# A feed-forward weight loaded in four column chunks instead of three, and two steps of the start put in another order

## The chip, the cores and the metric

The kernel runs on one core of a Trainium2 chip. The metric is the device time of one execution in microseconds (us); smaller is better. Engines are named as the profile names them: PE (TensorE matmul), PEld (its weight load), DVE (VectorE), ACT (ScalarE), POOL (GpSimd) and SP (SyncE). SPq, ACTq and POOLq are the instruction queues of those engines where they issue DMAs.

## The reference

`x` is 8 sequences of 4096 positions with 192 channels. The first step is a causal convolution along the sequence: the 192 channels are 8 heads of 24, each head has 7 taps, and the taps are softmaxed. The second step is a feed-forward layer over all 32768 rows, 192 to 2048 to 192, with an ELU between the two products.

```python
w = weight - np.max(weight, axis=-1, keepdims=True)
w = np.exp(w)
w = w / (np.sum(w, axis=-1, keepdims=True) + 1e-09)
x_pad = np.concatenate([np.zeros((B, K - 1, D), np.float32), x], axis=1)
x_unf = x_pad[:, np.arange(S)[:, None] + np.arange(K)[None, :], :].reshape(B, S, K, H, D // H)
att = np.einsum('hk,bskhg->bshg', w, x_unf).reshape(B * S, D)
h = att @ w_in                                     # 32768 x 2048
g = np.where(h > 0, h, np.exp(np.minimum(h, 0)) - 1)
out = g @ w_out                                    # 32768 x 192
```

`x`, `w_in` and `w_out` are float32 in DRAM. The kernel computes in 16-bit types with float32 accumulation; the DMAs that POOL issues convert while they load.

## The kernel before, in words

The 32768 rows are cut into 32 superblocks of 1024 rows, each of them two groups of 512. The hidden 2048 columns are cut into 16 strips `q` of 128 columns. One *pair* `n` is strip `q = n % 16` of superblock `s = n // 16`.

**One pair.** PE makes six matmuls into one of three slots of `H` (L646): three contraction steps `j` for each of the two groups `r`. The 192 channels are held as 3 times 64, and group 0 sits on partitions 0 to 63, group 1 on 64 to 127, so `w_in` has to be on chip twice, in the lower 64 partitions and in the upper 64. ACT takes the exponential of both groups (L437), POOL clamps it (L354), DVE makes `max(e - 1, h)` as `gT` (L500). A slot of `H` is free again when DVE is through, so PE is at most three slots ahead. A pair of PE instructions on zeroes (`warm_pair`, L537) stands before most pairs of the first superblock. The second product (L676) of superblock `t` is placed in the steps from pair `16 * (t + 1) - 1` on: in superblock 0 PE has nearly nothing to do but the pairs.

**The convolution.** For superblocks 1 on, PE multiplies windows of `x` (`xg`) by a band matrix of the taps, `Tr` (L619), ACT copies the result to `csb` (L417), SP writes it to DRAM (L713) and reads it back in the layout `att` that the pairs want (`read_att`, L279). The first two of these steps, `m = 0` and `m = 1`, stand in PE's order behind pairs 5 and 9; for them ACT copies the second half of the result only after the exponentials of the next pair (`late`). Pair 16 is the first that reads `att` from this way.

**The start.** Superblock 0 takes a shorter way, on chip. SP and ACT load the first 1024 rows as float32, `xf` (L249). ACT casts the first half to `xh` (L373, `s_xha`), DVE the second half (L482, `s_xh`). Meanwhile DVE has softmaxed the taps, PE spreads them over the partitions (L549, `s_wb`), and DVE multiplies them with a mask into seven diagonals `Dg` (L475, `s_D`). PE transposes `xh` (L556, L568), ACT and DVE copy the transposed blocks to `xT` (L375, L382, L484), PE applies the diagonals to `xT` (L588), ACT and DVE copy the result to `att` (L385, L391, L486, L491), and pair 0 can start. PE fills the time up to L549 with `WARM[0]` = 11 matmuls on zeroes (L532).

**The weight `w_in`.** It comes in chunks of columns (`WCOLS`), and `Q_PART` says which chunk strip `q` needs. Chunk 0 (columns 0 to 255, strips 0 and 1) is loaded from DRAM twice, once into each half of the partitions. Chunk 1 (256 to 1023, strips 2 to 7) and chunk 2 (1024 to 2047, strips 8 to 15) are loaded once, into the lower 64 partitions, by POOL's queue (L312, semaphores `s_w[1]`, `s_w[2]`); when such a chunk has landed, SP copies it to the upper 64 partitions with an on-chip DMA (L704, semaphores `s_wc`). PE waits for `s_w[0]`, or for the copy's semaphore, ahead of the first strip of each chunk.

**Queues.** POOL issues all converting loads one after the other before its first clamp: `w_in` chunk 0 twice, chunk 1, `xg` of superblock 1 in two parts (L307, parts 1 and 2), chunk 2, `xg` of superblock 2 part 1, the whole of `w_out` (L343), `xg` of superblock 2 part 2. SP issues in program order, and a wait holds everything behind it: the taps, one half of `xf`, the taps to DRAM (L695), the band `Tr` from them (L697), the two copies of `w_in`, then for `m = 0`: the write of `csb` (L713) and three reads of `att` (L279), then the same for `m = 1`, and so on through the kernel.

The order of PE, ACT and SP in the main part is one list, `order`, made when the program is built; it is the same before and after.

Of the kernel before, what the change touches and what calls it, by code (L numbers as in the profile page):

```python
# [12 lines left out]
P = 128  # L13
HP = 64
# [13 lines left out]
NE = 4  # L28
NG3 = 2
LAG = -1  # L30
WCOLS = ((0, 256), (256, 1024), (1024, 2048))
Q_PART = (0,) * 2 + (1,) * 6 + (2,) * 8
WARM = (11, 1)
HALF_STEPS = (10, 10, 6, 6, 10, 11, 11)

CONV_AT = ((4, 1, 1), (12, 2, 0))
# [15 lines left out]
def bass_lightweight_conv__then__act_elu_kernel(  # L52
# [55 lines left out]
    for n in range(NP + NQ + LAG):  # L108
        s, i = divmod(n, NQ)
# [25 lines left out]
    with ExitStack() as stack:  # L135
# [6 lines left out]
        def sema(name):  # L142
            return stack.enter_context(nc.semaphore(name))

        xh = sbuf("xh", [P, 2, QUAD, D], BF16)
# [24 lines left out]
        H = psum("H", [P, 3, 2 * GS])  # L170
        ops = psum("ops", [P, 2, GS])

        s_w = [sema(f"s_w{i}") for i in range(4)]
        s_wd = sema("s_wd")
        s_xl = [sema(f"s_xl{i}") for i in range(2)]
        s_xh = sema("s_xh")
        s_xha = sema("s_xha")
        s_wp = sema("s_wp")
        s_wb = sema("s_wb")
        s_wc = [sema(f"s_wc{i}") for i in range(2)]  # L180
        s_id = sema("s_id")
        s_one = sema("s_one")
        s_z0 = sema("s_z0")
# [99 lines left out]
        @block.gpsimd  # L283
        def _gpsimd(g: bass.BassGpSimd):
            W = Waits(g)

            def load_x(s, part):
                b, t0 = s % NXB, s * SUP
                first = s % SPB == 0
                if part == 0 and not first:  # L290
                    return
                if part == 0:
                    W(s_x[b][0], x_need[s, 0])
                    g.memset(xg[0:PAD, b, 0, :], 0.0).then_inc(s_z)
                    return
                if s > NXB:
                    W(s_cv, 2 * (s - NXB))
                if part == 1:
                    w0, w1, row = 0, XW, t0 - PAD
                else:  # L300
                    w0, w1, row = XW, NWIN, t0 + SUP - P - CW * (NWIN - 1 - XW)
                src = bass.AP(
                    tensor=x_flat.tensor,
                    offset=row * D,
                    ap=[[D, P], [CW * D, w1 - w0], [1, D]],
                )
                g.dma_start(xg[:, b, w0:w1, :], src).then_inc(s_x[b][part - 1], 16)  # L307

            def load_w_in(k, halves):
                c0, c1 = WCOLS[k]  # L310
                for r in halves:
                    g.dma_start(  # L312
                        w_in[HP * r : HP * (r + 1), :, c0:c1],
                        moe_w_in.rearrange("(p j) f -> p j f", j=3)[:, :, c0:c1],
                    ).then_inc(s_w[k], 16)

            W(s_one, 1)
            g.affine_select(
                out=ident[:],
                in_=ident[:],  # L320
                pattern=[[-1, P]],
                compare_op=ALU.is_equal,
                fill=0.0,
                base=0,
                channel_multiplier=1,
            ).then_inc(s_id)
            g.affine_select(
                out=sel[:].rearrange("p (r h c) -> p r h c", r=2, h=HEADS),
                in_=sel[:].rearrange("p (r h c) -> p r h c", r=2, h=HEADS),
                pattern=[[0, 2], [-1, HEADS], [0, 8]],  # L330
                compare_op=ALU.is_equal,
                fill=0.0,
                base=0,
                channel_multiplier=1,
            ).then_inc(s_id)
            W(s_wd, 16)
            load_w_in(0, (0, 1))
            load_w_in(1, (0,))
            for part in (1, 2):
                load_x(1, part)  # L340
            load_w_in(2, (0,))
            load_x(2, 1)
            g.dma_start(  # L343
                w_out[:, :, :], moe_w_out.rearrange("(q p) d -> p q d", p=FC)
            ).then_inc(s_w[3], 16)
            load_x(2, 2)
            for n in range(NP):
                s, i = divmod(n, NQ)
                for at, part in X_AT:
                    if at == i and s and s + NXB < NS:  # L350
                        load_x(s + NXB, part)
                for u in range(2):
                    W(s_exp, 2 * n + u + 1)
                    g.tensor_scalar(  # L354
                        out=E[:, n % NE, u, :],
                        in0=E[:, n % NE, u, :],
                        scalar1=1.0,
                        scalar2=0.0,
                        op0=ALU.min,
                        op1=ALU.max,  # L360
                    ).then_inc(s_clp)
# [85 lines left out]
        @block.vector  # L447
        def _vector(v):
            W = Waits(v)
            v.memset(zw[:], 0.0).then_inc(s_zw)  # L450
            v.memset(sel[:], 1.0)
            v.memset(ident[:], 1.0).then_inc(s_one)
            v.memset(xT[0:HP, :, :, 0:HALO], 0.0).then_inc(s_z0)
            v.memset(Dg[:, ::8, :], 0.0).then_inc(s_z0)
            v.memset(zt[:], 0.0).then_inc(s_z0)
            W(s_id, 1)
            v.tensor_tensor(mask[:], ident[:, 0:HP], ident[:, HP:P], ALU.add).then_inc(s_v)
            W(s_wd, 16)
            v.tensor_reduce(whm[:], wh[:], AXIS.X, ALU.max).then_inc(s_v)
            W(s_v, 2)  # L460
            v.tensor_scalar(
                out=wh2[:], in0=wh[:], scalar1=whm[:, 0:1], scalar2=None, op0=ALU.subtract
            ).then_inc(s_v)
            W(s_de, 1)
            v.reciprocal(whr[:], whs[:]).then_inc(s_v)
            W(s_v, 4)
            v.tensor_scalar(
                out=zt[:, CW - 1 : CW - 1 + KSIZE],
                in0=whe[:],
                scalar1=whr[:, 0:1],  # L470
                scalar2=None,
                op0=ALU.mult,
            ).then_inc(s_wp)
            W(s_wb, 1)
            v.tensor_tensor(  # L475
                Dg[:, 1:8, :],
                mask[:, :].unsqueeze(1).to_broadcast([P, KSIZE, HP]),
                H[:, 2, 0:KSIZE].unsqueeze(2).to_broadcast([P, KSIZE, HP]),
                ALU.mult,
            ).then_inc(s_D)  # L480
            W(s_xl[1], 16)
            v.tensor_copy(xh[:, 1, :, :], xf[:, 1, :, :]).then_inc(s_xh)  # L482
            W(s_tp, 3)
            v.tensor_copy(xT[:, 1, :, HALO : HALO + P], xt_bank(1)).then_inc(s_xtd)  # L484
            W(s_hc, 2)
            v.tensor_copy(  # L486
                att[:, 0, 1, :].rearrange("p (r t) -> p r t", r=2),
                H[:, 2, :].rearrange("p (r t) -> p r t", r=2)[:, :, 0 : GS // 2],
            ).then_inc(s_hd)
            W(s_hc, 3)  # L490
            v.tensor_copy(  # L491
                att[:, 0, 2, GS // 2 : GS], H[:, 0, GS : GS + GS // 2]
            ).then_inc(s_hd)
            for n in range(NP):
                s, q = divmod(n, NQ)
                if s >= NG3:
                    W(s_mm2, 2 * (s - NG3 + 1))
                for u in range(2):
                    W(s_clp, 2 * n + u + 1)
                    v.scalar_tensor_tensor(  # L500
                        out=gT[:, s % NG3, q, u, :],
                        in0=E[:, n % NE, u, :],
                        scalar=1.0,
                        in1=H[:, slot_of_pair[n] % 3, GS * u : GS * (u + 1)],
                        op0=ALU.subtract,
                        op1=ALU.max,
                    ).then_inc(s_tt)
            b = (2 * NS - 1) % 2
            W(s_mm2, 2 * NS)
            W(s_out[b], 32 * (NS - 1))  # L510
            v.tensor_copy(  # L511
                osb[:, b, 1, :, :].rearrange("p k d -> p (k d)"),
                H[:, last_slot % 3, GS : GS + 2 * D],
            ).then_inc(s_od)

        @block.tensor
        def _tensor(pe):
# [83 lines left out]
            for item in order:  # L601
# [26 lines left out]
                elif item[0] == "h":  # L628
# [5 lines left out]
                    elif n < NQ - 1 and not any(n - 2 <= e < n for e in EARLY_CONV):  # L634
                        conv_read(W, sum(e < n for e in EARLY_CONV) - 1)
                        warm_pair(WARM[1])
                    if Q_PART[q]:
                        W(s_wc[Q_PART[q] - 1], 16)
                    else:
                        W(s_w[0], 32)  # L640
                    W(s_att[s % 2], 16 * NDMA_ATT * ((s + 1) // 2))
                    k = slot_of_pair[n]
                    wait_slot(k)
# [10 lines left out]
                    ins.then_inc(s_h)  # L654
                else:
                    _, t, half, r0, r1 = item
                    W(s_w[3], 16)
                    if (t, half) == last_half:
                        acc = H[:, last_slot % 3, :].rearrange("p (g t) -> p g t", g=2)
                        if r0 == 0:  # L660
# [29 lines left out]
        def _sync(sy):  # L690
# [7 lines left out]
                Tr[:, :, :],  # L698
                bass.AP(tensor=taps.tensor, offset=0, ap=[[1, P], [ZW, HEADS], [1, CW]]),
            ).then_inc(s_band, 16)  # L700
            for k in (1, 2):
                c0, c1 = WCOLS[k]
                W(s_w[k], 16)
                sy.dma_start(  # L704
                    w_in[HP:P, :, c0:c1], w_in[0:HP, :, c0:c1]
                ).then_inc(s_wc[k - 1], 16)

            for item in order:
                if item[0] == "c":
# [52 lines left out]
```

## Time and profile before

| | us |
|---|---|
| median of four runs | 755.67 |
| lowest and highest | 754.07, 756.96 |
| the profiled execution, own time | 754.83 |
| its span (first to last instruction) | 753.1 |
| PE busy | 739.2 (98%) |
| ACT, POOL, DVE busy | 646.7, 658.5, 635.9 |
| L646 and L676 on PE, share of the chain that ended last | 44% each |

About 1.7 us of the profiled execution's own time lie outside the span. The span runs from 0; all places below are microseconds from there. In the list of busy time a row gives the source line, the engine, the operation, the tile written and the tiles read, how many there are, where the first starts and how long they cover. An entry in square brackets is the time in which the engine stood idle before, and what ended it.

### The profile page before, as it was taken

Reading aid. Unit: us, or ns where it says so; the run is one execution under the profiler, and the core shown is the slowest. Engines: PE = TensorE matmul, PEld = TensorE weight load, DVE = VectorE, ACT = ScalarE, POOL = GpSimd, SP = SyncE. Lnnn points to the kernel's source line nnn. Section 1 sums busy time; section 2 is a strip of 40 time slices with the busy share of each in tenths; the row PEclk is TensorE's granted clock in tenths of the full one; section 3 lists DMA queues with packets and bytes.
Section 4 is the critical chain, followed back from the end, with each engine's and each line's share of the span. In section 5 each row is a group of like instructions: output and inputs, shape, how many; then the busy total and the mean of one; then the engine's idle time right before and its main releaser. Section 6 shows DMA issues by size and latency. Waiting matters only on the chain.

```text
span 753.1 us, 32225 instructions
## 1 busy us (share of the span) xinstructions
PE 739.2 (98%) x13860; PEld 512.4 (68%) x13860; DVE 635.9 (84%) x1041; ACT 646.7 (86%) x1163; POOL 658.5 (87%) x1104
## 2 busy tenths in 40 slices
PE   6899999999999999999999999999999999999997
PEld 3366666667667667667667667767767767767676
DVE  3888898888898898898898898888888888888893
ACT  3888888888888888888888888888888888889882
POOL 5888898898998998998998998998998998998882
PEclk9999999999999999999999999999999999999999
DMA  9435345344345344345344345354355354355112
GB/s 178 101 86 109 81 101 117 78 102 98 92 102 114 78 103 95 95 102 113 78 105 95 92 104 111 77 107 93 90 108 110 74 111 92 88 112 106 59 44 64
DMA packets 106590, 72.79 MB, mean 97 GB/s; under 512 B 44488, under 2 KB 105808, under 8 KB 106448
## 3 DMA queue, kind: packets, MB, share of 16 engines
q1 hardware_dynamic: 66432, 54.77, 24.0%
q0 software_dynamic: 39600, 15.39, 19.1%
q8 instruction: 108, 1.77, 1.0%
q10 hardware_dynamic: 416, 0.59, 0.2%
q14 instruction: 34, 0.28, 0.1%
HBM read 44.00 MB, written 41.42 MB: 113 GB/s over the span
## 4 chain that ended last, share of the span: by engine, by line
PE 94%; DMA 2%; ACT 1%; DVE 1%; issue 0%; POOL 0%; SPq 0%
PE H L646 44%; PE ops L676 44%; PE H L619 5%; DMA w_in<-w_in 1%; DMA w_in<-in_moe_w_in_dram 1%; ACT E L437 1%; PE H L676 1%; DVE gT L500 1%; DMA att<-conv_slots 0%; DMA conv_slots<-csb 0%; ACT csb L417 0%; POOL w_in L312 0%; POOL E L354 0%; SPq L279 0%; PE ops L537 0%
## 5 line engine op out<-in xcount | busy, mean ns | idle before, releaser
L500 DVE SCALAR_TENSOR_TENSOR gT<-E,H 128x512 f16<-128x512 f32 x1024 | 630.5, 682 | 96.4 <-POOL E L354 88.5
L354 POOL TENSOR_SCALAR E<-E 128x512 f32<-128x512 f32 x1024 | 603.8, 612 | 79.4 <-ACT E L437 76.1
L437 ACT ACTIVATE E<-H 128x512 f32<-128x512 f32 x1024 | 546.1, 605 | 84.8 <-PE H L646 71.2
L676 PEld LDWEIGHTS ops<-w_out,gT 64*128 64x128 f16 x8064 | 342.1, 94 | 109.7 <-ACT osb L408 10.9
L676 PE MATMUL ops<-w_out,gT 64*128 64x192 f16 x8064 | 414.6, 243 | 0.9 <-DVE gT L500 0.9
L646 PE MATMUL H<-att,w_in 64*128 64x512 bf16 x3072 | 408.5, 378 | 5.1 <-DMA w_in<-w_in 2.4
L646 PEld LDWEIGHTS H<-att,w_in 64*128 64x128 bf16 x3072 | 130.3, 94 | 106.3 <-DVE gT L500 4.7
L417 ACT ACTIVATE csb<-H 128x1024 bf16<-128x1024 f32 x60 | 61.4, 1024 | 0.0
L408 ACT ACTIVATE osb<-ops 128x768 f32<-128x768 f32 x63 | 51.5, 817 | 5.1 <-PE ops L676 5.1
L307 POOL DMA_DIRECT2D xg<-in_x_dram x62 | 52.1, 841 | 0.4 <-issue 0.4
L619 PE MATMUL H<-Tr,xg 128*24 128x122 bf16 (+1 forms) x2400 | 39.3, 209 | 0.0
L619 PEld LDWEIGHTS H<-Tr,xg 128*24 128x24 bf16 x2400 | 30.1, 92 | 9.5 <-issue 9.5
L511 DVE COPY osb<-H 128x384 f32<-128x384 f32 x1 | 0.6, 558 | 8.9 <-PE H L676 8.9
L532 PE MATMUL ops<-zw 128*128 128x512 bf16 x11 | 4.5, 594 | 1.2 <-DVE zw L450 1.2
L676 PE MATMUL H<-w_out,gT 64*128 64x192 f16 x128 | 5.6, 243 | 0.1
L537 PE MATMUL ops<-zw 64*128 64x512 bf16 x20 | 4.4, 429 | 1.2 <-ACT csb L417 1.2
L676 PEld LDWEIGHTS H<-w_out,gT 64*128 64x128 f16 x128 | 5.2, 94 | 0.3 <-PE H L676 0.3
L400 ACT ACTIVATE osb<-H 128x384 f32<-128x384 f32 x1 | 0.5, 491 | 4.7 <-PE H L676 4.7
L532 PEld LDWEIGHTS ops<-zw 128*128 128x128 bf16 x11 | 1.5, 145 | 3.7 <-issue 2.5
L486 DVE CAST att<-H 128x512 bf16<-128x512 f32 x1 | 0.7, 692 | 3.3 <-PE H L588 3.3
L537 PEld LDWEIGHTS ops<-zw 64*128 64x128 bf16 x20 | 1.1, 105 | 3.4 <-ACT csb L417 2.2
L375 ACT ACTIVATE xT<-H 64x24 bf16<-64x24 f32 x1 | 0.2, 188 | 3.2 <-PE H L556 3.2
(46 smaller groups left out, 32.3 us busy)
## 6 DMA issues: line engine op xcount, KB each, us to landing
out_dram<-osb SPq DMA_DIRECT2D x127, 192.0 KB, 2.7
conv_slots<-csb SPq DMA_DIRECT2D x62, 256.0 KB, 2.5
att<-conv_slots SPq DMA_DIRECT2D x186, 64.0 KB
xg<-in_x_dram POOLq DMA_DIRECT2D x31, 240.0 KB, 5.1
xg<-in_x_dram POOLq DMA_DIRECT2D x31, 192.0 KB, 4.5
w_out<-in_moe_w_out_dram POOLq DMA_DIRECT2D x1, 768.0 KB, 16.4
xf<-in_x_dram ACTq DMA_DIRECT2D x1, 384.0 KB, 3.1
xf<-in_x_dram SPq DMA_DIRECT2D x1, 384.0 KB, 3.6
```

What stands on the lines that cost most here:

```text
L307: g.dma_start(xg[:, b, w0:w1, :], src).then_inc(s_x[b][part - 1], 16)
L354: g.tensor_scalar(out=E[:, n % NE, u, :], in0=E[:, n % NE, u, :], scalar1=1.0, scalar2=0.0, op0=ALU.min, op1=ALU.max,).then_inc(s_clp)
L408: a.activation(osb[:, b, :, :, :].rearrange("p g k d -> p g (k d)"), ops[:, :, 0 : 2 * D], ACT.Copy,).then_inc(s_oev)
L417: return a.activation(csb[:, m % 4, b0:b1, :], conv_bank(m)[:, b0:b1, :], ACT.Copy)
L437: a.activation(E[:, n % NE, u, :], H[:, k, GS * u : GS * (u + 1)], ACT.Exp).then_inc(s_exp)
L486: v.tensor_copy(att[:, 0, 1, :].rearrange("p (r t) -> p r t", r=2), H[:, 2, :].rearrange("p (r t) -> p r t", r=2)[:, :, 0 : GS // 2],).the ...
L500: v.scalar_tensor_tensor(out=gT[:, s % NG3, q, u, :], in0=E[:, n % NE, u, :], scalar=1.0, in1=H[:, slot_of_pair[n] % 3, GS * u : GS * (u + ...
L532: pe.matmul(ops[:, 0, :], zw[:, 0:P], zw[:], start=True, stop=True)
L537: pe.matmul(ops[:, r, :], zw[HP * r : HP * (r + 1), 0:P], zw[HP * r : HP * (r + 1), :], start=True, stop=True, tile_position=(HP * r, 0),)
L619: ins = pe.matmul(to[SLOT * q : SLOT * q + CPH, hb, o : o + nc_], xg[:, s % NXB, w, CPH * h : CPH * (h + 1)], Tr[:, h, CW - c0 - nc_ : CW ...
L646: ins = pe.matmul(H[:, k % 3, GS * r : GS * (r + 1)], w_in[HP * r : HP * (r + 1), j, FC * q : FC * (q + 1)], att[HP * r : HP * (r + 1), s ...
L676: ins = pe.matmul(acc[:, g, D * kb : D * (kb + 1)], gT[HP * rt : HP * (rt + 1), t % NG3, q, g, t0 : t0 + P], w_out[HP * rt : HP * (rt + 1) ...
```

## The change

`w_in` comes in four chunks: columns 0 to 255 (strips 0, 1), 256 to 639 (strips 2 to 4), 640 to 1279 (strips 5 to 9) and 1280 to 2047 (strips 10 to 15). The first three are loaded from DRAM into both halves of the partitions, and PE waits for both loads. The last is loaded into the lower half and copied to the upper half by SP, as before. So POOL issues seven loads of `w_in` in place of four, and part 2 of `xg` of superblock 1 goes behind the third chunk; SP issues one on-chip copy in place of two. On DVE the cast of the second half of the first `x` goes ahead of the multiplication that makes the diagonals. PE makes 9 matmuls on zeroes at the start in place of 11.

```diff
-WCOLS = ((0, 256), (256, 1024), (1024, 2048))
-Q_PART = (0,) * 2 + (1,) * 6 + (2,) * 8
-WARM = (11, 1)
+WCOLS = ((0, 256), (256, 640), (640, 1280), (1280, 2048))
+Q_PART = (0,) * 2 + (1,) * 3 + (2,) * 5 + (3,) * 6
+WARM = (9, 1)
...
-        s_w = [sema(f"s_w{i}") for i in range(4)]
+        s_w = [sema(f"s_w{i}") for i in range(5)]
...
-        s_wc = [sema(f"s_wc{i}") for i in range(2)]
+        s_wc = sema("s_wc")
...
             W(s_wd, 16)
             load_w_in(0, (0, 1))
-            load_w_in(1, (0,))
-            for part in (1, 2):
-                load_x(1, part)
-            load_w_in(2, (0,))
+            load_w_in(1, (0, 1))
+            load_x(1, 1)
+            load_w_in(2, (0, 1))
+            load_x(1, 2)
+            load_w_in(3, (0,))
             load_x(2, 1)
             g.dma_start(
                 w_out[:, :, :], moe_w_out.rearrange("(q p) d -> p q d", p=FC)
-            ).then_inc(s_w[3], 16)
+            ).then_inc(s_w[4], 16)
             load_x(2, 2)
...
             ).then_inc(s_wp)
+            W(s_xl[1], 16)
+            v.tensor_copy(xh[:, 1, :, :], xf[:, 1, :, :]).then_inc(s_xh)
             W(s_wb, 1)
             v.tensor_tensor(
                 Dg[:, 1:8, :],
...
             ).then_inc(s_D)
-            W(s_xl[1], 16)
-            v.tensor_copy(xh[:, 1, :, :], xf[:, 1, :, :]).then_inc(s_xh)
             W(s_tp, 3)
...
-                    if Q_PART[q]:
-                        W(s_wc[Q_PART[q] - 1], 16)
+                    if Q_PART[q] < 3:
+                        W(s_w[Q_PART[q]], 32)
                     else:
-                        W(s_w[0], 32)
+                        W(s_wc, 16)
...
-                    W(s_w[3], 16)
+                    W(s_w[4], 16)
...
-            for k in (1, 2):
-                c0, c1 = WCOLS[k]
-                W(s_w[k], 16)
-                sy.dma_start(
-                    w_in[HP:P, :, c0:c1], w_in[0:HP, :, c0:c1]
-                ).then_inc(s_wc[k - 1], 16)
+            c0, c1 = WCOLS[3]
+            W(s_w[3], 16)
+            sy.dma_start(w_in[HP:P, :, c0:c1], w_in[0:HP, :, c0:c1]).then_inc(s_wc, 16)
```

## The prediction

> **What bounds the kernel now.** I read the page first, then the chain that ended last, then the first 40 us instruction by instruction, the sums by stretch, and the DMA issues. Page:
>
> ```profile
> PE 739.2 (98%) x13860; PEld 512.4 (68%) x13860; DVE 635.9 (84%) x1041; ACT 646.7 (86%) x1163; POOL 658.5 (87%) x1104
> L646 PE MATMUL H<-att,w_in 64*128 64x512 bf16 x3072 | 408.5, 378 | 5.1 <-DMA w_in<-w_in 2.4
> w_out<-in_moe_w_out_dram POOLq DMA_DIRECT2D x1, 768.0 KB, 16.4
> ```
>
> PE is the bound of the whole, and the sums by stretch give it 702.41 of the 702.65 us between 37.35 and 740. The change touches nothing there. It can only move the moment at which this dense stretch begins: pair 16, at 37.35. Whatever that moves, the end moves by as much. So the start is read as a chain of its own; in the chain that ended last these are its pieces, start and length:
>
> ```profile
> 3.88 6.13 DMA w_in<-in_moe_w_in_dram
> 10.03 8.05 DMA w_in<-w_in
> 18.13 0.82 PE H L646 x6
> ...
> 31.52 2.12 DMA conv_slots<-csb
> ...
> 34.91 2.39 DMA att<-conv_slots
> ```
>
> Chunk 1 lands at 10.03, its copy takes 8.05, and only then pair 2 starts. From pair 2 the chain goes through the first superblock to the convolution behind pair 9, its DMAs and pair 16. The same in order of time:
>
> ```profile
> 5.90 0.62 DVE L475 TENSOR_TENSOR Dg<-mask,H 128x448 bf16<-128x448 bf16 x1 [2.32 <-PE H L549]
> 6.44 0.72 DVE L482 CAST xh<-xf 128x768 bf16<-128x768 f32 x1
> 7.30 0.53 PE L556 MATMUL H<-ident,xh 128*64 128x2 bf16 x9 [1.44 <-DVE xh L482]
> 13.86 0.82 PE L646 MATMUL H<-att,w_in 64*128 64x512 bf16 x6 [0.56 <-ACT att L391]
> 18.13 0.82 PE L646 MATMUL H<-att,w_in 64*128 64x512 bf16 x6 [2.36 <-DMA w_in<-w_in]
> 28.90 0.82 PE L646 MATMUL H<-att,w_in 64*128 64x512 bf16 x6
> 31.52 0.36 SPq L713 DMA_DIRECT2D conv_slots<-csb  x1
> 33.66 1.83 SPq L279 DMA_DIRECT2D att<-conv_slots  x3
> ```
>
> Two waits stand there: 1.44 us for the cast of `xh`, which DVE does behind the diagonals, and 2.36 us for the copy. The row at 28.90 is pair 10. Both waits halve the PE clock for a while (columns: stretch, length, PE busy, PEld, DVE, ACT, POOL, granted clock, DMA share, GB/s):
>
> ```profile
> 5.60:9.00 3.40, 1.65 (x38) 1.36 (x38) 1.75 (x3) 0.91 (x3) 3.40 (x5) 0.95 0.96 117
> 9.00:12.40 3.40, 3.38 (x36) 2.77 (x38) 0.20 (x1) 0.96 (x2) 0.63 (x1) 0.55 1.37 190
> 15.80:19.20 3.40, 1.07 (x10) 0.53 (x12) 2.48 (x4) 1.20 (x4) 1.96 (x4) 0.96 1.56 199
> 19.20:22.60 3.40, 3.40 (x20) 1.22 (x18) 1.95 (x4) 2.25 (x5) 2.38 (x4) 0.54 1.37 225
> 22.60:26.00 3.40, 2.77 (x58) 1.03 (x54) 2.97 (x6) 3.40 (x8) 2.91 (x5) 1.00 0.27 36
> ```
>
> After 1.65 and 1.07 us of work in 3.4 the next 3.4 us run near half rate; after 2.77 they do not. The DMA engines are full (share 1 or more) until about 22. Second loads are therefore not free; they take room from other loads.
>
> **Part 1, cast and diagonals turned, two warm matmuls fewer.** The second `xf` is issued at 1.26 and takes 3.6 us (DMA issues), so it is there at 4.86. DVE stood idle 2.32 us ahead of `Dg`; the cast now takes 4.86 to 5.58. Two of 11 warm matmuls in 4.51 us are 0.82, so L549 runs near 4.9, and `Dg` 5.6 to 6.2, well before L588 wants it. The transposes start 0.14 after the cast as before, at 5.7 in place of 7.30: 1.6 us. If the stretch 5.6 to 9.0 is now busy (1.4 us of transposes and 1.6 of L588), the halved clock on L588 goes too, up to 3.4 x 0.5 = 1.7 us. Pair 0 starts at 12.3 or, with the clock, 10.6.
>
> **Part 2, chunks 1 and 2 (strips 2 to 9) loaded twice.** Chunk 1 now has two times 144 KB, the 288 KB that one half had, in the same place of POOL's queue: both halves are there near 10.0, and pair 2 (14.1 or 12.4) waits no more. The 2.36 us go, with the half clock on pairs 3 to 5. Chunk 2 lands behind 192 + 288 + 240 + 480 = 1200 KB, less than the 1296 KB behind which the old chunk 2 landed at 17.0 (SP's two copy issues cover 10.03 to 17.58, and one takes 0.6), so by about 16.5. Pair 5 wants it once DVE is through with pair 2: DVE starts 2.19 after pair 0 and takes 1.25 a pair (10 instructions in 6.12), so 16.6 to 18.3. Part 2 of `xg`, 192 KB later, is there near 18; its user, the convolution behind pair 9, starts past 22. POOL issues three loads more, 3 x 0.64 = 1.9 us, and is through at 11.6 in place of 9.6; its first clamp comes 1.55 after pair 0, at 12.1 or later. That cover is thin; gone, it would cost 1 us at most, ahead of a wait that hides it.
>
> **Part 3, chunk 3, what is late next.** Strip 10 needs the copied half. Ahead of it POOL's queue has 1200 + 192 + 288 = 1680 KB, 384 KB (393,000 bytes) more than before. Between 10.03 and 17.03 (DMA queues of that stretch) that queue moved 0.96 MB, 137 GB/s, and with SP's 0.45 MB 201 GB/s. So the load lands 2.0 to 2.9 us after 17.0; with full credit for the first copy's 295,000 bytes that are gone, 0.5. I take 2.0, at 19.0. Then the copy: 8.05 for 288 KB behind `Tr` on SP's queue, 6.8 for 384 KB (issue to landing), where 2,457,000 bytes of float32 (`xg`, `w_out`, `xg`) were still to come, just as now. I take 6.8, being the same neighbour: 25.8. Bounds: 17.5 + 6.3 (a quarter fewer bytes) = 23.8, and 19.9 + 8.1 = 28.0.
>
> Unhindered, pair 10 would start when DVE is through with pair 7, 12.7 us after pair 0 (2.19 + 8 x 1.25 + 0.5 for the two convolution copies on ACT): 23.3 or 25.0. So the copy is what ends last, and parts 1 and 2 are hidden behind it, save for what they bring up to there. Pair 10 moves from 28.90 to 25.8: 3.1 us won.
>
> **From pair 10 to pair 16.** The second half of `csb` for `m = 1` comes after pair 10's exponentials, 2.6 us after its start, so the write, the reads and pair 16 follow pair 10 rigidly. Two things take a little back. SP's write for `m = 0` lies behind the copy in one queue: it lands near 26.8 (256 KB, estimated 1 us at the rates above), the three reads then take 2.1 of issue, and the write for `m = 1` can go at 28.9, where its data are there at 28.4: 0.4 lost. And PE stands idle 1 to 2 us ahead of pair 10, so pair 10 may run at half rate: 0.64 (0.82 became 1.5 there), from nothing to this. They overlap; I take 0.5 for both. On every engine the later work is the same.
>
> Sum: 754.83 - 3.1 + 0.5 = 752.3. That is against the profiled execution, which lies 0.84 under the median. I don't add it: the places where the phase of the clock can cost (L588, pairs 3 to 5) now lie ahead of the copy and are hidden by it.
>
> **Two rules of the Trainium skill.** "SBUF — State Buffer", section "Can I just issue two DMAs to hit both halves?", says that loads to the two halves of the partitions serialize on the same 16 engines, measured there at 6% over one: this speaks against the change. The full DMA share above agrees. By its 196 GB/s for a transfer of 64 partitions, 393,000 bytes would cost an estimated 2.0 us, and the sum would stay at 752.3. "TensorE: Matmul & The Clock Gate", Part 1, says that the clock halves after an idle window of about 3.4 us; here 1.07 to 1.65 us of work in such a window did not save it. By the page the wait of 1 to 2 us at pair 10 halves nothing, and the sum would be 752.2.
>
> **Rivals.**
> (a) The copy is not late: it lands by 23 to 24, since chunk 3 has the first copy's room to itself. Pair 10 starts at 23.3 to 25.0 by DVE: 5.6 to 3.9 won, 749.2 to 750.9. For: the lower bound 23.8. Against: both copies took 6.8 or more.
> (b) The copy is late by the upper bound, 28.0: pair 10 wins 0.9, the chain takes 0.5 back: 754.4, no change.
> (c) Slower: SP's queue gets through only when POOL's queue is empty. For: before, the second copy landed at 23.8, close to `w_out` at 7.70 + 16.4 = 24.1. With 2.9 us more of loads that emptying is at 27.0, last `xg` behind it 28.0, then the copy's own bytes (1.5 at 201 GB/s) and a landing of about 1: 30.5. Pair 10 is 1.6 late, the half clock adds 0.6: 757.1. It decides from a landing past 28.3. Against: the first copy landed at 18.08, in the middle of POOL's loads.
>
> **How the numbers follow.** Forecast 0.57, (a) 0.18, (b) 0.15, (c) 0.10. A change under 0.3% (2.3 us) can't be told from none here, so the border to "faster" is 753.4. Of the forecast's own range, 750.8 to 754.0 (copy at 24.3 to 27.5), some three quarters lie under it, and all of (a): 0.43 + 0.18 = 0.61. Slower takes (c) almost whole, 0.08. The range reaches from the middle of (a), 749.6, to past (b), 755.4.
>
> **What would show it.** The wait of L646 for `w_in<-w_in` moves from pair 2 to pair 10, 1 to 2.5 us long; transposes at 5.7; pair 0 before 12.4; pair 2 without a wait; the copy issued near 19 and landing near 26; one stretch of half clock near 26; pair 16 near 34.8. Wrong would be: no wait at pair 10 (then lower), a copy past 28, or a wait at pair 5 for chunk 2 or ahead of the first convolution for `Tr`, longer than what the copy hides.

## The result, and the profile after

The changed kernel takes 753.18 us (median of 43 executions, 750.79 to 754.31), the kernel before 754.55 (63 executions): a ratio of 0.9974, 95% interval 0.9968 to 0.9981. The gain is clear, but it is 0.26%, under the 0.3% that the prediction drew as its border. The profiled execution of the changed kernel took 751.81, 3.0 us less than the profiled one of before, with a span of 750.1 in place of 753.1.

The lines that answer to those shown of before, first from the page of the changed kernel:

```profile
PE 737.8 (98%) x13858; PEld 511.8 (68%) x13858; DVE 635.7 (85%) x1041; ACT 646.8 (86%) x1163; POOL 660.4 (88%) x1107
w_out<-in_moe_w_out_dram POOLq DMA_DIRECT2D x1, 768.0 KB, 14.7
```

Then its chain that ended last, in order of time (start, length):

```profile
1.26 3.57 DMA xf<-in_x_dram
4.85 0.64 DVE xh L476
...
12.31 0.84 PE H L647 x6
...
14.51 6.08 DVE gT L501 x10
...
22.26 3.75 DMA conv_slots<-csb
26.02 0.67 SPq L279
...
27.98 2.46 DMA conv_slots<-csb
...
31.71 2.56 DMA att<-conv_slots
```

No piece of it is `w_in` any more. The chain starts with the load of the first `x`, runs through the cast that was turned, then at DVE's pace, and from 22.26 on through SP's queue: the write for `m = 0`, its reads, the write for `m = 1`, its reads. The same in order of time:

```profile
5.63 0.61 PE L557 MATMUL H<-ident,xh 128*64 128x2 bf16 x9 [0.24 <-DVE xh L476]
12.31 0.82 PE L647 MATMUL H<-att,w_in 64*128 64x512 bf16 x6 [0.57 <-ACT att L392]
14.03 0.83 PE L647 MATMUL H<-att,w_in 64*128 64x512 bf16 x6
17.94 0.73 SPq L704 DMA_DIRECT2D w_in<-w_in  x1
24.88 0.82 PE L647 MATMUL H<-att,w_in 64*128 64x512 bf16 x6
34.31 0.82 PE L647 MATMUL H<-att,w_in 64*128 64x512 bf16 x6 [1.47 <-DMA att<-conv_slots]
```

The first two rows are the transposes and pair 0, then come pair 2, the copy on SP, pair 10 and pair 16. The transposes wait 0.24 us for the cast (1.44 before). Pair 2, at 14.03, waits for nothing (2.36 before). The copy is issued at 17.94 and takes 6.2, so it is there at 24.1, and pair 10 starts at 24.88 without a wait for it. Pair 10 is 4.0 us earlier than before, pair 16 only 3.0: its wait for `att` has grown from 0.41 to 1.47.

### The profile page after: what moved, and what is told of

Read it like the earlier page. It is cut to its first block, busy times and chain, and to the rows that moved or that the text cites. A ratio compares the mean times of both kernels' runs of the same rounds, so it can differ in the third digit from the quotient of the medians.

```text
span 750.1 us, 32224 instructions
## 1 busy us (share of the span) xinstructions
PE 737.8 (98%) x13858; PEld 511.8 (68%) x13858; DVE 635.7 (85%) x1041; ACT 646.8 (86%) x1163; POOL 660.4 (88%) x1107
## 4 chain that ended last, share of the span: by engine, by line
PE 95%; DMA 2%; DVE 1%; ACT 1%; SPq 0%; issue 0%; POOL 0%
PE ops L677 44%; PE H L647 44%; PE H L620 5%; DVE gT L501 1%; DMA conv_slots<-csb 1%; PE H L677 1%; DMA xf<-in_x_dram 0%; ACT E L438 0%; SPq L279 0%; DMA att<-conv_slots 0%; PE H L589 0%; POOL E L355 0%; PE ops L589 0%; PE H L569 0%; PE H L557 0%
## 5 line engine op out<-in xcount | busy, mean ns | idle before, releaser
L312 POOL DMA_DIRECT2D w_in<-in_moe_w_in_dram x7 | 4.6, 657 | 0.3 <-DMA wh<-in_weight_dram 0.3
```

The costliest lines, as they stand in the source:

```text
L312: g.dma_start(w_in[HP * r : HP * (r + 1), :, c0:c1], moe_w_in.rearrange("(p j) f -> p j f", j=3)[:, :, c0:c1],).then_inc(s_w[k], 16)
```

## The experiments

The kernels ran in three groups, each on one chip beside the kernel before: e1, e2, e3 and e4 (before: 756.12), a2, e5, e6 and e7 (755.29), and a3, e2b, e7b and e8 (755.45). The changed kernel itself was in the second group (a2) and the third (a3), not in the first. What the profiled execution of each showed, in us (a place is left empty where the profile has both writes in one row):

| kernel | pair 0 | pair 10, its wait for `w_in` | write for m = 1 issued | pair 16, its wait for `att` | span | span less pair 16 |
|---|---|---|---|---|---|---|
| before | 13.86 | 28.90, none | 31.52 | 37.35, 0.41 | 753.1 | 715.8 |
| changed | 12.31 | 24.88, none | 27.98 | 34.31, 1.47 | 750.1 | 715.8 |
| changed (a2) | 11.17 | 24.42, 0.78 | 27.89 | 34.64, 2.33 | 751.7 | 717.1 |
| changed (a3) | 11.19 | 25.18, 1.51 | 28.37 | 34.88, 1.81 | 750.6 | 715.7 |
| e1 | 11.21 | 29.76, none | 32.38 | 38.27, 0.47 | 754.0 | 715.7 |
| e2 | 12.61 | 25.18, none | 27.94 | 34.89, 1.75 | 750.6 | 715.7 |
| e2b | 11.74 | 24.80, 0.58 | 28.02 | 34.64, 1.96 | 751.7 | 717.1 |
| e3 | 12.32 | 24.89, 0.2 | 27.43 | 33.56, 0.71 | 749.3 | 715.7 |
| e4 | 12.47 | 25.05, none | 28.43 | 35.48, 2.47 | 751.2 | 715.7 |
| e5 | 11.30 | 24.55, 0.79 | 27.70 | 34.53, 2.10 | 750.1 | 715.6 |
| e6 | 11.11 | 29.80, none | 32.26 | 38.16, 0.47 | 753.9 | 715.7 |
| e7 | 10.73 | 23.80, none | | 31.55, none | 747.2 | 715.7 |
| e7b | 10.90 | 25.14, 1.87 | | 33.56, none | 749.3 | 715.7 |
| e8 | 13.94 | 26.51, none | | 34.52, none | 750.2 | 715.7 |

The last column is the frame for all that follows: from pair 16 to the end it is 715.6 to 715.8 us in 12 of 14 profiles, and 717.1 in two. What moves pair 16 moves the end by as much.

### e1: the start alone

The kernel before, with the start of the changed one:

```diff
-WARM = (11, 1)
+WARM = (9, 1)
...
+            W(s_xl[1], 16)
+            v.tensor_copy(xh[:, 1, :, :], xf[:, 1, :, :]).then_inc(s_xh)
             W(s_wb, 1)
...
-            W(s_xl[1], 16)
-            v.tensor_copy(xh[:, 1, :, :], xf[:, 1, :, :]).then_inc(s_xh)
```

> The kernel before with the start of the changed one: cast ahead of the diagonals and 9 warm matmuls, w_in as before. Theory (the start is hidden whenever a w_in wait comes later): pair 0 starts near 12.3 in place of 13.86, pair 2 still waits for the copy that lands near 18.1, now about 3.9 us, pair 16 stays at 37.3 and the time is that of before within 0.5 us. Rival (the start's 1.55 us reach the end by themselves): pair 16 near 35.8, 1.5 us faster than before.

Measured: 755.38, ratio 0.9991 (0.9981 to 1.0001). In order of time:

```profile
11.21 0.82 PE L646 MATMUL H<-att,w_in 64*128 64x512 bf16 x6 [0.56 <-ACT att L391]
18.42 1.46 PE L646 MATMUL H<-att,w_in 64*128 64x512 bf16 x6 [5.31 <-DMA w_in<-w_in]
38.27 0.82 PE L646 MATMUL H<-att,w_in 64*128 64x512 bf16 x6 [0.47 <-DMA att<-conv_slots]
```

Pair 0 came 2.65 us earlier, and all of it went into the wait of pair 2, now 5.31 us. Pair 16 was even 0.9 later: the copy landed 0.3 later, and after the longer idle time the clock was halved for some 6.8 us (pair 2 took 1.46 in place of 0.82). The start by itself is worth nothing that this can tell.

### e2 and e2b: the chunks alone

The changed kernel, with the start of before:

```diff
-WARM = (9, 1)
+WARM = (11, 1)
...
-            W(s_xl[1], 16)
-            v.tensor_copy(xh[:, 1, :, :], xf[:, 1, :, :]).then_inc(s_xh)
             W(s_wb, 1)
...
+            W(s_xl[1], 16)
+            v.tensor_copy(xh[:, 1, :, :], xf[:, 1, :, :]).then_inc(s_xh)
             W(s_tp, 3)
```

> The changed kernel with the start of before: diagonals ahead of the cast and 11 warm matmuls. Theory (with chunks loaded twice DVE's pace from pair 0 on sets pair 10): pair 0 at 13.9, pair 10 near 26.4 without a wait for w_in, SP no later than its data, pair 16 near 35, 2.4 us faster than before and 0.6 slower than the changed kernel. Rival (the recorded forecast, the copy of the last chunk sets pair 10): pair 10 where the changed kernel has it, near 24.9 or where the copy lands, and the same time as the changed kernel.

> The changed kernel with the start of before, on the same chip as the changed one. Theory (the start is hidden by the copy and by SP's way): pair 0 0.5 to 1.5 us later than in the changed kernel, pair 16 within 0.6 us of it, the time within 0.6 us of it. Rival (the start reaches the end): the time 1.2 to 1.6 us over the changed kernel's.

Measured: 752.61, ratio 0.9957 (0.9941 to 0.9974), and 753.43, 0.9968 (0.9957 to 0.9980). The changed kernel's three ratios are 0.9974, 0.9966 and 0.9953. In e2 pair 10 had no wait for the copy, as its theory said, though pair 0 came at 12.61 and not at 13.9. On the one chip that had both (third group), the chunks alone were 1.5 us slower than the changed kernel, which speaks for the rival of e2b; but in the profiles pair 16 stood at 34.64 against the changed kernel's 34.88, so there the start had not reached pair 16. What differed between these two profiles is the last column, 717.1 against 715.7: a half clock behind pair 16, as the next section shows. That doesn't explain the times, though: two of e2b's six executions have a granted clock of 1.000 over the whole span, so no such stretch, and took 753.45 and 753.55, against 751.55 to 752.40 for the three of a3 with the same 1.000. The chunks carry the change. Whether the start adds something in the mean is not settled by these runs; the times of the third group speak for it.

### a2 and a3: the changed kernel again

> The changed kernel itself, for a comparison on one chip and for a second look at its start. Theory (the first change of the PE clock falls anywhere in 3.4 us and sets where pair 0 starts): pair 0 between 11.2 and 12.4, pair 10 without a wait for w_in 12.6 later, pair 16 at 33.2 to 34.4 with a wait of 1.2 to 1.7 us for att. Rival (the start is fixed): pair 0 at 12.3 again.

> The changed kernel again, beside the next three on one chip. Theory (in it the start reaches no further than the copy and SP's way for att): pair 0 anywhere from 10.7 to 12.4, pair 16 within 34.2 to 34.7 all the same.

Measured: 752.81, ratio 0.9966 (0.9953 to 0.9978), and 751.93, 0.9953 (0.9939 to 0.9966). Two parts of a2's expectation missed: pair 10 did wait for the copy, and pair 16 came at 34.64 after a wait of 2.33, past 34.4 and 1.7. Pair 16 of a3, at 34.88, is just past its range too. The first profile shows one of two cases, a2 and a3 the other. From a2, in order of time:

```profile
7.79 1.06 PE L589 MATMUL ops<-xT,Dg 64*128 64x256 bf16 x16 [0.33 <-ACT xT L383]
11.17 0.82 PE L647 MATMUL H<-att,w_in 64*128 64x512 bf16 x6 [0.56 <-ACT att L392]
24.42 1.47 PE L647 MATMUL H<-att,w_in 64*128 64x512 bf16 x12 [0.78 <-DMA w_in<-w_in]
34.64 0.82 PE L647 MATMUL H<-att,w_in 64*128 64x512 bf16 x6 [2.33 <-DMA att<-conv_slots]
```

The first 16 matmuls of L589 took 1.06 us. In the first profile of the changed kernel the same row says 1.89, in a stretch whose granted clock (last figure but two) reads 1.00:

```profile
7.66 1.89 PE L589 MATMUL ops<-xT,Dg 64*128 64x256 bf16 x16
5.60:9.00 3.40, 3.37 (x50) 2.86 (x52) 1.14 (x2) 1.39 (x3) 3.40 (x6) 1.00 1.05 143
```

By these durations the PE clock had gone to full before them in a2, and only after them there. So pair 0 came at 11.2 in place of 12.3, pair 10 was ready sooner than the copy and waited for it, 0.78 us here and 1.51 in a3. Pair 16 nevertheless came within 0.6 us of the first profile's: what the earlier clock gave was taken back by the copy and by SP's way for `att`. The sums by stretch behind pair 16, of a2 and then of the first profile of the changed kernel (stretch, length, PE, PEld, DVE, ACT, POOL, granted clock, DMA share, GB/s):

```profile
32.90:36.40 3.50, 1.76 (x52) 1.25 (x56) 1.29 (x3) 0.90 (x2) 0.70 (x2) 0.94 0.12 31
36.40:39.80 3.40, 3.40 (x48) 2.30 (x42) 1.28 (x2) 2.08 (x4) 1.17 (x3) 0.55 0.23 77
```

```profile
32.90:36.40 3.50, 2.08 (x64) 1.51 (x66) 1.82 (x4) 1.46 (x4) 1.56 (x3) 1.00 0.12 35
36.40:39.80 3.40, 3.33 (x52) 2.04 (x50) 2.42 (x4) 2.99 (x5) 2.25 (x5) 1.00 0.22 77
```

After the wait of 2.33 us the clock was halved for 3.4 us in which PE had no slack, and a2's span has 1.4 us more behind pair 16 than the other. e2b shows the same in the stretch from 35.4 to 38.8 (granted clock 0.56), and the same 717.1. No other profile does. The 43 times of the changed kernel fit two groups: 15 from 750.8 to 752.0, 28 from 752.7 to 754.3, none between. That the second group is the executions with the halved clock behind pair 16 is argued from the profiled executions (753.4 and 753.4 with it; 751.81, 752.40, 752.36 and 751.87 without, counting e2 and e5), not shown for each. The mean granted clock of each execution agrees: 3.4 us at half rate take 0.0023 off the mean of a span of 750, and it reads 0.999 or 1.000 in all 15 of the first group and 0.997 to 0.999 in 26 of the 28 of the second. It doesn't say where in the span a half stretch lies, and two executions of the second group have 1.000. Nor is it the whole difference: the middles of the groups, 751.30 and 753.60, lie 2.3 us apart, and the halved stretch made 1.4.

### e5: eleven warm matmuls

```diff
-WARM = (9, 1)
+WARM = (11, 1)
```

> The changed kernel with 11 warm matmuls in place of 9. Theory (the transposes stand behind the warm matmuls in PE's order): L550 ends near 6.1, the transposes start at 6.1 in place of 5.6, pair 0 is 0.4 us later at the same phase of the clock and the time 0.2 to 0.5 us longer. Rival (the longer warm-up brings the full clock one window earlier): pair 0 up to 1 us earlier, the time up to 0.7 us shorter.

Measured: 752.93, ratio 0.9964 (0.9951 to 0.9977), beside 0.9966 for the changed kernel on the same chip. The transposes started at 6.17, against 6.07 and 6.09 in a2 and a3, where the second half of `xf` landed only near 5.4. The two warm matmuls less are worth nothing measurable; neither the theory's 0.2 to 0.5 us nor the rival's earlier clock is seen.

### e6: the copied chunk wanted two pairs earlier

```diff
-WCOLS = ((0, 256), (256, 640), (640, 1280), (1280, 2048))
-Q_PART = (0,) * 2 + (1,) * 3 + (2,) * 5 + (3,) * 6
+WCOLS = ((0, 256), (256, 640), (640, 1024), (1024, 2048))
+Q_PART = (0,) * 2 + (1,) * 3 + (2,) * 3 + (3,) * 8
```

> The changed kernel with the border between the third chunk and the copied one at column 1024 in place of 1280, so that strips 8 to 15 need the copy (384 KB) in place of 10 to 15. Theory (the copy lands near 24 whatever its size, and a pair that wants it earlier than that waits): pair 8 waits 1 to 2 us for w_in<-w_in at a place where it would start at 22.5, pair 16 is 0.8 to 1.5 us later than in the changed kernel and the time as much longer. Rival (SP's way for att ends last at pair 16 anyway and hides the wait): a wait at pair 8, but pair 16 and the time within 0.3 us of the changed kernel.

Measured: 754.84, ratio 0.9989 (0.9980 to 0.9999): 2.0 us slower than the changed kernel on the same chip, nearly all of the gain gone. In order of time, the copy, pair 8 and pair 16:

```profile
19.00 0.72 SPq L704 DMA_DIRECT2D w_in<-w_in  x1
25.89 1.46 PE L647 MATMUL H<-att,w_in 64*128 64x512 bf16 x6 [4.41 <-DMA w_in<-w_in]
38.16 0.82 PE L647 MATMUL H<-att,w_in 64*128 64x512 bf16 x6 [0.47 <-DMA att<-conv_slots]
```

The copy took 6.85 and landed near 25.85, whoever waits for it; pair 8 waited 4.41 us, the clock was halved (pair 8 took 1.46), and in this profile pair 16 was 3.5 us later than in a2. The direction was as expected, the size more than the 0.8 to 1.5 us expected. In this kernel a copied chunk has to begin at a strip that is wanted later than about 25 us.

### e4: no copy at all

```diff
...
-            load_w_in(3, (0,))
+            load_w_in(3, (0, 1))
...
-                    if Q_PART[q] < 3:
-                        W(s_w[Q_PART[q]], 32)
-                    else:
-                        W(s_wc, 16)
+                    W(s_w[Q_PART[q]], 32)
...
-            c0, c1 = WCOLS[3]
-            W(s_w[3], 16)
-            sy.dma_start(w_in[HP:P, :, c0:c1], w_in[0:HP, :, c0:c1]).then_inc(s_wc, 16)
```

> The changed kernel with the last chunk loaded into both halves too, and no on-chip copy at all. Theory (the copy is in time, only its place in SP's queue ahead of the write for m = 0 costs something): pair 10 stays at 24.9, the write for m = 0 lands before 26, pair 16 at 33.4 to 34.3, the time from that of the changed kernel to 0.9 us less. Rival (288 KB more in POOL's queue keep the DMA engines full longer and hold up SP's write): w_out lands 1.5 to 2 us later, the write for m = 0 lands past 27, pair 16 past 35, at least 0.7 us slower than the changed kernel.

Measured: 753.66, ratio 0.9966 (0.9955 to 0.9978), beside e3's 0.9932 on the same chip. In order of time:

```profile
22.42 0.36 SPq L704 DMA_DIRECT2D conv_slots<-csb  x1
26.46 1.93 SPq L278 DMA_DIRECT2D att<-conv_slots  x3
28.43 0.45 SPq L704 DMA_DIRECT2D conv_slots<-csb  x1
35.48 0.82 PE L643 MATMUL H<-att,w_in 64*128 64x512 bf16 x6 [2.47 <-DMA att<-conv_slots]
```

Without a copy ahead of it the write for `m = 0` landed no earlier, at 26.46 in place of 26.02. POOL's loads are the likeliest thing that holds it. Between 24 and 26 the DMA share (last figure but one) was 0.66 here and 0.19 in the changed kernel, first e4, then the changed kernel:

```profile
24.00:26.00 2.00, 1.76 (x50) 0.74 (x46) 2.00 (x4) 2.00 (x6) 1.95 (x5) 1.00 0.66 154
```

```profile
24.00:26.00 2.00, 1.60 (x48) 0.74 (x46) 2.00 (x5) 2.00 (x5) 1.95 (x4) 1.00 0.19 49
```

So a price of the copy's place in SP's queue is not seen, but e4 took the copy out and put 288 KB of loads in, and the two are not separated. The rival's direction held in the profile (pair 16 at 35.48, 0.6 to 1.2 later than in the three profiles of the changed kernel); its sizes did not (`w_out` landed at 24.7, 0.4 later and not 1.5 to 2, the write at 26.46 and not past 27), and by time the ratio is inside the range of the changed kernel's on other chips.

### e3: SP's reads for m = 0 behind the write for m = 1

```diff
-                    if m == 0 or g == 1:
-
+                    if m == 1:
+                        read_att(sy, W, 1, 0)
+                    if g == 1:
                         read_att(sy, W, s, g)
```

> The changed kernel with one thing moved on SP: the three reads for m = 0 go behind the write for m = 1. Theory (1 us between pair 10 and pair 16 is lost because SP waits for the write of m = 0 and issues its reads before the write of m = 1): the write for m = 1 is issued at 27.4 in place of 27.98, pair 16 starts at 33.3 to 33.8 in place of 34.31, the time is 0.5 to 1.0 us under the changed kernel's. Rival (the DMA rings are busy then, whatever SP's order): the write takes longer by what it starts earlier, pair 16 at 34.2 or later, the same time.

Measured: 750.88, ratio 0.9932 (0.9918 to 0.9946), beside 0.9957 and 0.9966 for e2 and e4 on the same chip. In order of time:

```profile
27.43 0.36 SPq L711 DMA_DIRECT2D conv_slots<-csb  x1
27.83 3.79 SPq L279 DMA_DIRECT2D att<-conv_slots  x6
33.56 0.82 PE L647 MATMUL H<-att,w_in 64*128 64x512 bf16 x6 [0.71 <-DMA att<-conv_slots]
```

The write for `m = 1` goes when its data are there, at 27.43, and pair 16 comes 0.75 us earlier than in the first profile of the changed kernel, where pair 0 and pair 10 stood at the same places. So that part of the gain was lost on SP, by the order of its queue: behind a write that took 3.75 us to land, three reads of 0.6 us issue each, and then a write that was issued right behind these reads and took 2.46 (2.1 in the kernel before, e1 and e6, where it was issued 0.9 to 3.1 us after the last of them). That running beside the reads is what made it slower is argued; no run changed that alone.

### e7, e7b and e8: the same with m = 1 one pair earlier, and the start of before in it

e7 and e7b are e3 with this; e8 has in addition the order of cast and diagonals and the 11 warm matmuls of before, as in e2:

```diff
-EARLY_CONV = {5: (1, 0), 9: (1, 1), 16: (2, 0)}
+EARLY_CONV = {5: (1, 0), 8: (1, 1), 16: (2, 0)}
```

> The kernel with SP's reads for m = 0 behind the write for m = 1, and the convolution m = 1 behind pair 8 in place of pair 9. Theory (pair 16 still waits 0.7 us for att there, and the way of m = 1 can start 1.2 us earlier): the write for m = 1 is issued near 26.3, pair 16 starts at 32.8 to 33.2 limited by a slot of H, the time is 0.4 to 0.7 us under that kernel's and 1.2 to 1.6 under the changed one's. Rival (POOL's loads fill the DMA engines until 25 and what is issued earlier lands no earlier): pair 16 near 33.5, no gain.

> The kernel with SP's reads for m = 0 late and m = 1 behind pair 8, again, on the same chip as the changed one: 2 to 3 us faster than it.

> The same kernel (reads late, m = 1 behind pair 8) with the start of before: diagonals ahead of the cast, 11 warm matmuls. Theory (once neither the copy nor SP's way holds up the pairs, DVE's pace from pair 0 on carries the start through to pair 16): pair 0 0.5 to 1.5 us later, pair 16 and the time later by as much, where the copy is in time. Rival (the turned order of cast and diagonals is worth nothing anywhere): the time within 0.3 us.

Measured: e7 750.16, ratio 0.9927 (0.9913 to 0.9942), and 750.98, 0.9933 (0.9917 to 0.9948): faster than both kernels, 2.65 us under the changed one in the second group (1.2 to 1.6 were expected), but only 0.95 in the third, where 2 to 3 were expected. e8 752.30, ratio 0.9959 (0.9946 to 0.9972). Pair 10 and pair 16 of e7, pair 10 of e7b, pairs 0 and 16 of e8, each in order of time:

```profile
23.80 0.82 PE L647 MATMUL H<-att,w_in 64*128 64x512 bf16 x6 [0.71 <-DVE gT L501]
31.55 0.82 PE L647 MATMUL H<-att,w_in 64*128 64x512 bf16 x6
```

```profile
25.14 0.98 PE L647 MATMUL H<-att,w_in 64*128 64x512 bf16 x6 [1.87 <-DMA w_in<-w_in]
```

```profile
13.94 0.82 PE L647 MATMUL H<-att,w_in 64*128 64x512 bf16 x6 [0.56 <-ACT att L392]
34.52 0.81 PE L647 MATMUL H<-att,w_in 64*128 64x512 bf16 x6
```

Pair 16 has no wait for `att` left. By these profiles the copy now decides: in e7 it was issued at 17.35 and in time, in e7b at 18.61 and 1.87 us late, and pair 16 stood at 31.55 and 33.56. With the start of before the median was 1.3 us over e7b's on the same chip (the intervals of the two ratios overlap by a hair), and in the profile e8's pair 16 was 1.0 us behind e7b's and 3.0 behind e7's. The rival, that the earlier start is worth nothing anywhere, fits badly. But the theory, that SP's way hides it before, isn't shown by this: with SP's order left as it was, e2b lay as far (1.5 us) over a3.

## Why the prediction was right or wrong

The forecast was 752.3, 749.6 to 755.4, and 753.18 lies in the range. (Its own terms, 754.83 - 3.1 + 0.5, make 752.23.) Against the profiled execution before, the sum was 2.5 us won; the profiled execution won 3.0, the medians 1.4. The chance of 0.61 for more than 0.3% went to the wrong side of that border. The border of 753.4 had been reckoned from 755.67, the median of four executions; from the 754.55 of 63 it is 752.3. That the sum comes so near has some luck in it: pair 10 won 4.0 us in place of 3.1, the way from there to pair 16 lost 1.0 in place of 0.5, and the two misses have opposite signs.

**What bounds, and where the gain ends up: right.** The dense stretch from pair 16 on lasts 715.7 us whatever the start does, in all profiles but two. Pair 16 was forecast near 34.8 and stood at 34.31, 34.64 and 34.88.

**Part 1: right in size, hidden not in every case.** The transposes were forecast at 5.7, and pair 0 at 12.3 or, with the clock, 10.6. They came at 5.63 to 6.09, and pair 0 at 12.31, 11.17 and 11.19. e1 shows it hidden by the copy of the old chunk. Behind the new copy it was hidden in a2 and a3, but not at pair 10 of the first profile, which DVE's pace from pair 0 set; and the times of e2b and e8 lie 1.5 and 1.3 us over those with the new start. Also, the prediction bound the clock to the stretch 5.6 to 9.0 being busy or not. In the first profile that stretch was busy for 3.37 of 3.40 us, and L589's first matmuls were slow all the same. It is the place of the first full clock that differs between executions of the same kernel, before L589 or behind its first 16 matmuls.

**Part 2: right.** Pair 2 and pair 5 wait for no load of `w_in` in any profile of the changed kernel (pair 5 waits 0.25 us for DVE). POOL's three more issues delayed nothing: its first clamp, at 13.87, waited for ACT.

**Part 3, the copy that ends last: the step that was half right.** It said that the copy lands at 25.8 and that pair 10 waits for it, against 25.0 or 23.3 by DVE's pace. The term that was mis-sized is the landing: the load of the last chunk landed at 17.94 and 18.75 (19.0 forecast), and the copy took 6.2 to 6.4 (6.8 forecast), 24.1 to 25.1 in all. So in the first profile, with the late clock, pair 10 had nothing to wait for, as in rival (a); the prediction had named this as a sign that it was wrong, with a lower time. In a2 and a3, with the early clock, it waited 0.78 and 1.51 for the copy, as in the forecast. The second loads cost about the 2.0 us of the sum or less: 384 KB more went ahead of the last chunk, and it landed 0.9 to 1.75 us after the old one's 17.0 (16.2 in e1, which loads as before; from there it is 1.7 to 2.6). In the first profile `w_out` behind them landed at 24.3 in place of 24.1.

**From pair 10 to pair 16: the mechanism right, the size too small.** Pair 16 came 8.45 us after pair 10 before and 9.43 after the change: 1.0 lost, where the sum has 0.5. SP's write for `m = 1` waited for its turn behind the reads for `m = 0`, as the prediction said with 0.4 us; e3, which takes this out, measured 0.75. It was missed that the write itself then took 2.46 in place of 2.12.

**The clock: looked for at the wrong wait.** The prediction charged up to 0.64 us for a half clock at pair 10. No half clock followed that pair in the three profiles of the changed kernel. But it put no half clock behind the wait at pair 16, and said of everything later that it is the same. That is the step that failed: in a2, behind a wait of 2.33 us there, the clock was halved in the dense stretch, 1.4 us. If the grouping of the times is read rightly, this befalls most of the 28 of 43 executions in the second group, and it is a part of why the medians gained 1.4 and not 3; some 0.9 of the 2.3 us between the groups stays open.

**Rivals (b) and (c): not seen.** No profile of the changed kernel had the copy past 25.2. Whether SP's copy gets through only as POOL's loads run out stays open: in the first profile it landed at 24.1 and `w_out` at 24.3, but that end came only 0.2 us later than before, so the price that (c) put on it was not there.

**The two rules of the Trainium skill.** That loads to the two halves of the partitions share the same engines ("SBUF — State Buffer", "Can I just issue two DMAs to hit both halves?") agrees in direction: e4, which loads still more in this way, has a fuller DMA share (0.66 against 0.19 between 24 and 26) and a later pair 16. No run set two half loads beside one load of the same bytes. That it takes an idle window of about 3.4 us to halve the clock ("TensorE: Matmul & The Clock Gate", Part 1) did not hold here: a2's clock halved after a wait of 2.33 us, behind a stretch in which PE was busy for 1.76 of 3.50.

## What to carry to other kernels

Follow a chain to the next point where something else joins it, and give every joining chain its own arrival time and spread: here three chains (DVE's pace, an on-chip copy, a queue of small DMAs) came within 1 to 2 us of each other, so 1.0 of the 4.0 us won at pair 10 was gone at pair 16. An in-order DMA queue that must wait for a write before it issues that write's reads holds up later writes; issuing the next write first won 0.75 us here (e3). And a new wait of 2 us is dearest at the edge of a dense stretch, where the PE clock can halve afterwards and nothing hides it (1.4 us in a2).

## What the runs showed that was not expected

- The same code reached pair 0 at 11.2 or at 12.3, as the clock went to full before L589 or behind its first 16 matmuls (1.06 against 1.89 us for these). The column of the granted clock does not tell: for the changed kernel it says 1.00 in the stretch 5.60 to 9.00, in which those 16 matmuls took 1.89. It seems to hold nothing ahead of the first change that was recorded; the durations of like matmuls are the safer reading.
- A wait of 2.33 us at pair 16 was followed by a halved clock (a2), and so was one of 1.96 (e2b); waits of 2.10 (e5) and 2.47 (e4) at the same place were not. The Trainium skill ("TensorE: Matmul & The Clock Gate", Part 1) says that the window in which PE's activity is counted runs freely and isn't reset when a kernel starts. That waits of like length end in either way fits that, but no run here moved the window alone.
- A copy on SP's queue took 6.2 to 8.1 us from issue to landing for 288 to 384 KB while POOL's loads filled the engines. The 256 KB write of `csb` took 2.1 us in the kernel before, where it was issued at 26.36. In the ten profiles in which the write for `m = 0` was issued between 20.7 and 22.6 it landed between 25.7 and 27.1, so issuing it earlier brought next to nothing; the last of POOL's loads landed near 25.4 in the first profile of the changed kernel. This is near to what rival (c) supposed of SP's queue, though the copy itself, landing at 24.1, did not wait for that end.
- Doubling the loads of half of `w_in` moved `w_out`, near the end of POOL's queue, by only 0.2 us, and the last load behind it by 0.3. The on-chip copies shrank by the same 384 KB, from 672 to 288, so this isn't the price of the loads alone.
